# A fused attention and gated feed-forward kernel: other transfers, another order and other engines for the first four packs

## The chip, the cores and the metric

The kernel runs on one core of a Trainium2 chip. That core has a matrix engine (TensorE, PE in the profile), three engines for elementwise work (VectorE or DVE, ScalarE or ACT, GpSimd or POOL), a queue engine that only issues transfers (SyncE, SP), and 16 DMA engines. ScalarE and GpSimd can issue transfers too. Each engine takes its instructions in the order in which they stand in its program and waits at the first one whose semaphores are not there yet. The metric is the device time of one execution in microseconds; smaller is better.

## The reference, cut to what matters

The inputs are q, k and v (8 sequences, 8 heads, 576 positions, 64 values) and three weight matrices. Half of the heads see the last 32 positions, the other half every fourth of the last 128. The result of the attention is the input x of a gated feed-forward network, all in float32.

```python
def _attn_ref(q, k, v) -> np.ndarray:
    ...
    window = 32
    dilation = 4
    ...
    mask_plain = (rel >= 0) & (rel < window)
    mask_dil = (rel >= 0) & (rel < window * dilation) & (rel % dilation == 0)
    ...
    attn = np.exp(scores)
    attn = attn / (np.sum(attn, axis=-1, keepdims=True) + 1e-09)
    return np.matmul(attn, v).astype(np.float32)

def _moe_ref(x, w_gate, w_val, w_out) -> np.ndarray:
    g = x @ w_gate
    silu = g * (1.0 / (1.0 + np.exp(-g)))
    val = x @ w_val
    return (silu * val @ w_out).astype(np.float32)
```

x has 4608 tokens of 512 values; the hidden width is 1536.

## The kernel before

**Tiling.** Tokens are cut into packs of 256 tokens and 4 heads, and three chunks of 512 tokens are made in a plain way, the rest in three larger chunks that use seven products in place of eight. A pack goes through these stages: its scores (TensorE, on top of a mask that a matmul with the identity has put there), a shift by the row maximum (VectorE), the exponential (ScalarE), a transposition on TensorE and its copy out by ScalarE, the results with v (TensorE), a division by the row sum and a 32 by 32 transposition that puts them where x lies (VectorE).

**Two parts for each number.** Matmuls of the network run on a shorter format. Each factor is split: the high part is a copy into that format (ScalarE), the low part is the number less its high part (GpSimd, `x_copy_lo` at L502, `w_split_lo` at L267, and L558 for the hidden values h). A product takes three matmuls, high by high, low by high, high by low. Weights come in 24 units of 128 by 768 numbers of 8 bytes, of which five stages make two parts: E (an exponent part, ScalarE, L225), T (a shift, ScalarE at L242 or VectorE at L245), B (the bits joined, VectorE, L252 or L255), H (the high part, ScalarE, L263), L (the low part, GpSimd, L267). Step s of the plain chunks needs units 2s and 2s + 1: 12 matmuls for the gate, 12 for the value, 12 of the step before for the output.

**The first four packs.** They have functions of their own (`first_...`). Their q takes both head halves in turn over the 128 partitions; their k and v lie in places of double width that are cleared, half by half, before the rows of one half are written into them, so that one matmul serves both halves. `first_qk` issues three transfers for a pack: q over 128 partitions, and k for each half over 64. `first_v` issues two.

**What sets the order.** The loads of this stage stand in one block, and the engine that clears and the one that issues are named in the calls. The work of the first packs and of the first weight units is a list of tokens, which each engine gets in that order: a letter names the stage, a number the pack, or for W the weight stage (W0 is E, W4 is L, each on the next unit). Q is scores, S shift, X exponential, T transposition, K its copy, A results, N division, U the 32 by 32 transposition, H and L the two parts of x, Y and Z dummy matmuls. After the list the steps of the plain chunks follow; their order is laid down by the program's text and by a scheduler that reads it. At most 8 transfers of SP and ACT together are under way in this stage: each one's semaphore is that of the eighth before it, and it waits for that one to land.

Of the kernel before, what the change touches and what calls it, by code (L numbers as in the profile page):

```python
# [18 lines left out]
P = 128  # L19
# [96 lines left out]
def attention_moe(ctx, tc, qkb, vb, w, masks, ident, out):  # L116
# [3 lines left out]
    def pk(m):  # L120
        return PACKS[m]
# [143 lines left out]
    def w_split_lo(u):  # L265
        hi, lo = w_place(u)
        nc.gpsimd.tensor_tensor(out=lo, in0=wst.pop(u).bitcast(F32), in1=hi, op=ALU.subtract)  # L267
# [10 lines left out]
    def w_one(c):  # L278
        u = done[c]
        done[c] += 1  # L280
        if c == "E":
            w_exp(u)
        elif c == "T":
            w_shift(u)
        elif c == "B":
            w_bits(u)
            while ready["w"] and w_load():
                pass
        elif c == "H":
            w_split_hi(u)  # L290
        else:
            w_split_lo(u)
# [7 lines left out]
    FQ = max(2 * x.cols - FQN for x in PACKS[:4])  # L300
# [8 lines left out]
    for k, n in (("qk", FQ), ("v", 8 * FG * (D + 1))):  # L309
        early[k] = Ring(n, *range(o, o + 4 * n, n))  # L310
        o += 4 * n
# [188 lines left out]
    def x_copy_lo(m):  # L500
        h, l = x_parts(m)
        nc.gpsimd.tensor_tensor(out=l, in0=x_place(m), in1=h, op=ALU.subtract)  # L502
# [97 lines left out]
    with tc.manual_schedule(engines={et.SP, et.Pool, et.DVE, et.Activation}):  # L600
# [406 lines left out]
def layout(q, k, v, moe_w_gate, moe_w_val, moe_w_out):  # L1007
# [4 lines left out]
    for m, pk in enumerate(PACKS):  # L1012
        for (g, h), t in pk.blocks.items():
# [37 lines left out]
```

## Time and profile before

| | |
|---|---|
| median of 3 runs | 911.01 us (910.01 to 911.1) |
| the profiled execution | 910.72 us, of which the span of the program is 908.9 us |
| busy: PE, DVE, ACT, POOL | 898.4, 651.6, 375.0, 272.3 us |
| granted TensorE clock | 1.00 |
| DMA moved | 203.90 MB, 224 GB/s over the span |

The profile is of one execution, and its times are microseconds from the start of the span. Four kinds of answers are used: the busy time of each engine in stretches of the span; the timeline of one engine (start, duration, engine, line, operation, what it writes and reads, shapes, count, and in brackets how long the engine was idle before and what it waited for); the waits by engine and line; and the chain that ended last, followed back from the last instruction. `fs` is the bank of scores, `fk` and `ek` those of transposed rows, `fr` and `er` those of results, `bg`, `bv` and `bo` those of the gate, the value and the output. A DVE instruction of 0.96 us on 128 by 768 elements is one stage of a weight unit.

### The profile page before, as it was taken

The numbers are of one execution on the slowest core, as the hardware profiler recorded it, in microseconds if no ns is written. First come the engines' busy times: TensorE is split into PE (matmuls) and PEld (weight loads), VectorE is DVE, ScalarE is ACT, GpSimd is POOL, SyncE is SP. The second block draws the span as 40 slices with busy tenths as digits, with TensorE's granted clock in tenths as the row PEclk, the third lists the DMA queues.
The fourth block names the chain that finished last, engine by engine and source line by source line (L and its number), as shares of the span: only waits on it lengthen the run. The fifth ranks groups of instructions, "written<-read, shape, count | busy, mean of one in ns | idle before, by whom it ended". The sixth has DMA issues, their size and how long they took to land.

```text
span 908.9 us, 19519 instructions
## 1 busy us (share of the span) xinstructions
PE 898.4 (99%) x8082; PEld 732.1 (81%) x8082; DVE 651.6 (72%) x1014; ACT 375.0 (41%) x593; POOL 272.3 (30%) x311
## 2 busy tenths in 40 slices
PE   8899999999999999999999999999999999999998
PEld 5588888888888878888888888888888888888886
DVE  7766638788797983776689966677699746556963
ACT  6776623322333242333345543333354533334451
POOL 4766531231111122232333121232333213333310
PEclk9999999999999999999999999999999999999999
DMA  9975416776696765787777878777776776666672
GB/s 347 353 254 225 155 50 205 242 246 243 207 320 231 238 227 181 251 257 225 226 222 227 259 233 258 222 234 243 238 208 200 226 230 199 188 196 198 186 220 104
DMA packets 72553, 203.90 MB, mean 224 GB/s; under 512 B 7408, under 2 KB 21744, under 8 KB 72464
## 3 DMA queue, kind: packets, MB, share of 16 engines
q0 software_dynamic: 27520, 100.16, 36.7%
q1 hardware_dynamic: 35728, 66.32, 20.4%
q10 hardware_dynamic: 9216, 36.17, 11.7%
q8 instruction: 64, 1.05, 0.5%
q14 instruction: 25, 0.20, 0.1%
HBM read 160.15 MB, written 42.47 MB: 223 GB/s over the span
## 4 chain that ended last, share of the span: by engine, by line
PE 89%; DVE 4%; DMA 3%; issue 1%; SPq 1%; ACT 1%; POOL 1%; DVEq 0%; ACTq 0%; POOLq 0%
PE bo L853 33%; PE bv L853 12%; PE bg L853 12%; PE bo L566 9%; PE bg L517 9%; PE bv L517 9%; PE two L454 2%; PE two L414 2%; DMA pieces<-at_float32r 2%; PE two L440 1%; DMA at_int<-w 1%; DMA at_float<-vb 1%; SPq L752 0%; DVE at_float32r L744 0%; DVE at_float L730 0%
## 5 line engine op out<-in xcount | busy, mean ns | idle before, releaser
L853 PE MATMUL bo<-at_float32r 128*128 128x512 f32 x1296 | 307.5, 391 | 0.0
L853 PEld LDWEIGHTS bo<-at_float32r 128*128 128x128 f32 x1296 | 242.1, 188 | 50.9
L782 POOL DMA_DIRECT2D at_float32r<-pieces x189 | 101.6, 538 | 358.5 <-PE bo L853 223.0
L816 DVE TENSOR_TENSOR at_float<-bo,at_float 128x512 f32<-128x512 f32 (+1 forms) x169 | 113.4, 683 | 100.0 <-ACT at_float L858 59.2
L816 DVE TENSOR_TENSOR at_float32r<-at_float,at_float32r 128x512 fp32r<-128x512 f32 (+1 forms) x147 | 110.8, 778 | 31.5 <-ACT at_float32r L843 24.1
L853 PE MATMUL bg<-at_float32r 128*128 128x512 f32 x486 | 128.8, 391 | 0.0
L853 PE MATMUL bv<-at_float32r 128*128 128x512 f32 x486 | 128.8, 391 | 0.0
L566 PE MATMUL bo<-at_float32r,at_float32r 128*128 128x512 f32 x432 | 105.7, 393 | 0.8 <-POOL at_float32r L558 0.4
L558 POOL TENSOR_TENSOR at_float32r<-at_float,at_float32r 128x512 fp32r<-128x512 f32 x36 | 51.7, 1437 | 182.5 <-PE bo L566 120.6
L853 PEld LDWEIGHTS bv<-at_float32r 128*128 128x128 f32 x486 | 90.6, 188 | 19.0
L853 PEld LDWEIGHTS bg<-at_float32r 128*128 128x128 f32 x486 | 90.6, 188 | 18.7
L517 PE MATMUL bg<-at_float32r,at_float32r 128*128 128x512 f32 x420 | 102.7, 393 | 0.9 <-POOL at_float32r L267 0.5
L843 ACT CAST at_float32r<-at_float 128x512 fp32r<-128x512 f32 x126 | 75.7, 622 | 65.6 <-PE bo L853 16.2
L517 PE MATMUL bv<-at_float32r,at_float32r 128*128 128x512 f32 x420 | 102.7, 393 | 0.0
L566 PEld LDWEIGHTS bo<-at_float32r,at_float32r 128*128 128x128 f32 x432 | 80.1, 188 | 18.5 <-POOL at_float32r L558 0.8
L517 PEld LDWEIGHTS bg<-at_float32r,at_float32r 128*128 128x128 f32 x420 | 77.8, 188 | 18.3 <-DVE at_float L543 1.0
L517 PEld LDWEIGHTS bv<-at_float32r,at_float32r 128*128 128x128 f32 x420 | 77.8, 188 | 16.5
L879 ACT ACTIVATE at_float<-at_float 128x512 f32<-128x512 f32 x72 | 45.5, 632 | 93.0 <-DVE at_float L816 93.0
L858 ACT COPY at_float<-bg 128x512 f32<-128x512 f32 x63 | 37.0, 587 | 91.3 <-PE bg L853 91.1
L543 DVE SCALAR_TENSOR_TENSOR at_float<-at_float,bg 128x512 f32<-128x512 f32 x36 | 24.6, 682 | 58.8 <-ACT at_float L538 49.5
L816 POOL TENSOR_TENSOR at_float<-at_float,at_float 128x512 f32<-128x512 f32 x36 | 50.8, 1410 | 23.8 <-DVE at_float L882 20.3
L881 DVE SCALAR_TENSOR_TENSOR at_float<-at_float,at_float 128x512 f32<-128x512 f32 x72 | 49.4, 687 | 11.6 <-ACT at_float L879 11.5
(85 smaller groups left out, 882.4 us busy)
## 6 DMA issues: line engine op xcount, KB each, us to landing
at_float32r<-pieces POOLq DMA_DIRECT2D x189, 512.0 KB, 4.5
pieces<-at_float32r SPq DMA_DIRECT2D x126, 256.0 KB, 3.3
at_int<-w SPq DMA_DIRECT2D x24, 768.0 KB, 7.5
at_float<-vb ACTq DMA_DIRECT2D x31, 520.0 KB, 5.1
at_float<-qkb ACTq DMA_DIRECT2D x16, 640.0 KB, 7.0
out<-at_float SPq DMA_DIRECT2D x35, 256.0 KB, 4.2
at_float<-qkb ACTq DMA_DIRECT2D x15, 576.0 KB, 6.2
at_float<-vb SPq DMA_DIRECT2D x6, 260.0 KB, 8.2
```

The lines of the kernel that those rows point to most:

```text
L414: nc.tensor.matmul(out=two[BQ * j:BQ * j + BQ, h, a + w * g:a + w * g + w], lhsT=t[r, q:q + BQ], rhs=t[r, k:k + w], start=not masked, stop ...
L517: last["g", which] = nc.tensor.matmul(out=bank.rearrange("p (n c) -> p n c", n=2), lhsT=wcol(f, o, low), rhs=x[l][j], start=n == 0, stop=n ...
L543: last["h"] = nc.vector.scalar_tensor_tensor(out=t, in0=t, scalar=1.0, in1=bank_g[:, :CH], op0=ALU.add, op1=ALU.mult)
L558: last["l"] = nc.gpsimd.tensor_tensor(out=hl, in0=hst[i][0], in1=hst[i][1], op=ALU.subtract)
L566: nc.tensor.matmul(out=bank_o[j][:, :CH], lhsT=wcol(f, 2 * DM + P * j, low), rhs=x, start=f == 0 and low == 0 and x is hh, stop=f == NF - ...
L782: nc.gpsimd.dma_start(out=taken[asked], in_=pieces[asked % NPIECE])
L816: engine.tensor_tensor(out=out, in0=a, in1=b, op=op)
L843: nc.scalar.copy(out=o[:, 0], in_=src)
L853: nc.tensor.matmul(out=bank, lhsT=w, rhs=x, start=first and n == 0 and t in FRESH, stop=last and n == len(ops) - 1, skip_group_check=True)
L858: nc.scalar.copy(out=kept[KEPT[t]][r], in_=banks[0][r][:, :CS])
L879: nc.scalar.activation(out=f, in_=g, func=AF.Tanh, scale=0.5)
L881: nc.vector.scalar_tensor_tensor(out=f, in0=f, scalar=1.0, in1=g, op0=ALU.add, op1=ALU.mult)
```

## The change

Four things change, all in the first stage.

1. *Joined transfers.* The host lays q beside k for one half and k beside q for the other, so that one row of a half holds both, and the place is as wide as both. `first_qk` issues two transfers for a pack, of 64 partitions and 1152 or 1280 columns, in place of three. The place's columns between belong to q of both halves; the k columns of the other half are cleared as before. The same bytes are moved.
2. *Who clears and who issues.* Clears are calls of their own (`first_clear`), by VectorE and GpSimd, ahead of the transfers. The second half of q and k is issued by ScalarE (before: GpSimd for packs 0 to 2, SP for pack 3), the second half of v by GpSimd for all packs (before: SP for packs 2 and 3). ScalarE clears one half instead of four, and issues the identity that SP issued.
3. *Low parts.* Those of x for packs 2 and 3 (token D) and of the first two weight units (token V) are made by VectorE.
4. *The list of tokens* is written anew.

```diff
-    def first_qk(m, zero, engine):
-
-        t, n = early["qk"](), pk(m).cols
-        k = n - FN
-        tk = t[:, FN:FN + 2 * k].rearrange("p (h c) -> p h c", h=2)
-        nc.sync.dma_start(out=t[:, :FN], in_=qkb[m, :, :FN])
+    def first_clear(what, m, by):
+
+        k = pk(m).cols - FN
+        t = early[what](2 * (k + FN) if what == "qk" else None).rearrange("p (h c) -> p h c", h=2)
         for h in range(2):
-            clear(tk[:, h], zero[h])
-            (nc.sync, engine)[h].dma_start(out=tk[h::2, h], in_=qkb[m, D * h:D * h + D, FN:n])
-        st[m]["qk"] = t[:, :FN], tk
+            clear(t[:, h, :k] if what == "qk" else t[:, h], by[h])
+        st[m][what] = t
+
+    def first_qk(m, engine):
+
+        t, k = st[m]["qk"].rearrange("p h c -> p (h c)"), pk(m).cols - FN
+        for h in range(2):
+            engine[h].dma_start(out=t[h::2, k * h:k * h + FN + k], in_=qkb[m, D * h:D * h + D, :FN + k])
+        st[m]["qk"] = t[:, k:k + FN], st[m]["qk"]
...
-    def x_copy_lo(m):
+    def x_copy_lo(m, engine=nc.gpsimd):
         h, l = x_parts(m)
-        nc.gpsimd.tensor_tensor(out=l, in0=x_place(m), in1=h, op=ALU.subtract)
+        engine.tensor_tensor(out=l, in0=x_place(m), in1=h, op=ALU.subtract)
...
-        first_qk(0, (dve, pool), pool)
         nc.scalar.dma_start(out=consts[:, :near], in_=masks[:, :near])
-        first_qk(1, (dve, pool), pool)
-        nc.sync.dma_start(out=ident32, in_=ident)
+        for m in range(3):
+            first_clear("qk", m, (dve, pool))
+        first_qk(0, (sp, act))
+        first_qk(1, (sp, act))
         nc.scalar.activation(out=some, in_=some, func=AF.Exp)
 
         idle(WARM)
-        first_qk(2, (dve, pool), pool)
-        first_v(0, (dve, pool), pool)
-        first_qk(3, (dve, act), sp)
-        first_v(1, (dve, pool), pool)
+        first_qk(2, (sp, act))
+        nc.scalar.dma_start(out=ident32, in_=ident)
+        for m in range(2):
+            first_clear("v", m, (dve, pool))
+            first_v(m, (sp, pool))
+        first_clear("qk", 3, (dve, pool))
+        first_qk(3, (sp, act))
         w_load()
-        first_v(2, (dve, act), sp)
-        first_v(3, (act, act), sp)
+        for m in range(2, 4):
+            first_clear("v", m, ((dve, act)[m - 2], pool))
+            first_v(m, (sp, pool))
         w_load()
...
-        "L": x_copy_lo, "Y": idle, "Z": lambda n: idle(n, s_banks[0]), "W": lambda n: w_one(STAGES[n]),
+        "L": x_copy_lo, "D": lambda m: x_copy_lo(m, nc.vector), "V": lambda n: w_one(STAGES[n], nc.vector),
+        "Y": idle, "Z": lambda n: idle(n, s_banks[0]), "W": lambda n: w_one(STAGES[n]),
...
-        for what in ("Q0 S0 Q1 Y2 S1 X0 Q2 X1 T0 S2 T1 K0 K1 Q3 X2 A0 T2 K2 S3 X3 N0 A1 W0 U0 T3 K3 N1 A2 W1 U1 H0 L0 H1 L1 "
-                     "W2 Z2 A3 N2 W3 W4 U2 W0 Z3 H2 L2 N3 W1 U3 H3 L3 W2 W0 W3 W4 W0 W1 W2 W3 W4").split():
+        for what in ("Q0 S0 Q1 X0 S1 Q2 T0 K0 S2 X1 A0 T1 X2 N0 K1 T2 U0 K2 A1 H0 L0 N1 Q3 U1 S3 Z3 H1 L1 W0 X3 T3 W1 A2 K3 N2 W2 Z2 A3 "
+                     "W3 U2 W0 Z3 N3 V4 H2 W1 U3 D2 H3 W2 W0 D3 W3 V4 W0 W1 W2 W3 W4").split():
```

How this moves instructions, at the three places of which the prediction speaks.

TensorE from the third pack's scores on, before (L362 are scores, L440 transpositions, L380 results; each row's first name is the bank, `fk` or `fr` for even packs, `ek` or `er` for odd ones):

```order
L362 MATMUL fs_109<-at_2048_float_146 32x128 x16
L440 MATMUL fk<-at_128_float_59,at_512_float_216 128x128 x4
L440 MATMUL ek<-at_128_float_59,at_512_float_239 128x128 x4
L358 LDWEIGHTS at_1056_bfloat_58
L358 MATMUL fs_113<-at_1056_bfloat_58 128x512
L362 MATMUL fs_113<-at_2048_float_157 32x128 x16
L380 MATMUL fr<-at_2080_float_152,at_512_float_216 32x130 x16
L440 MATMUL fk<-at_128_float_59,at_512_float_265 128x128 x4
L380 MATMUL er<-at_2080_float_163,at_512_float_239 32x130 x16
L440 MATMUL ek<-at_128_float_59,at_512_float_313 128x128 x4
L380 MATMUL fr<-at_2080_float_170,at_512_float_265 32x130 x16
```

The same piece now (L364 scores, L442 transpositions, L382 results):

```order
L364 MATMUL fs_109<-at_2560_float_129 32x128 x16
L442 MATMUL fk<-at_128_float_59,at_512_float_212 128x128 x4
L382 MATMUL fr<-at_2080_float_149,at_512_float_212 32x130 x16
L442 MATMUL ek<-at_128_float_59,at_512_float_234 128x128 x4
L442 MATMUL fk<-at_128_float_59,at_512_float_259 128x128 x4
L382 MATMUL er<-at_2080_float_154,at_512_float_234 32x130 x16
L360 LDWEIGHTS at_1056_bfloat_58
L360 MATMUL fs_113<-at_1056_bfloat_58 128x512
L364 MATMUL fs_113<-at_2560_float_159 32x128 x16
```

Results of pack 0 stand ahead of the transposition of pack 1, and the scores of pack 3 behind the results of pack 1. Three dummy matmuls, the transposition of pack 3 and the results of pack 2 follow.

VectorE from the bits of the first weight unit on, before (L388 to L390 are the division, L487 the 32 by 32 transposition, L252 the bits of a unit, L245 and L255 shift and bits of the third):

```order
L252 SCALAR_TENSOR_TENSOR at_776_int_367<-at_1536_int_168 128x3x256
L388 TENSOR_SCALAR at_8_float_317<-fr 128x8
L389 RECIPROCAL at_8_float_317<-at_8_float_317 128x8
L390 TENSOR_TENSOR at_512_float_318<-fr,at_8_float_317 128x512
L487 STREAM_TRANSPOSE at_512_float_400<-at_512_float_318 128x2x4x2x32
L388 TENSOR_SCALAR at_8_float_346<-er 128x8
L389 RECIPROCAL at_8_float_346<-at_8_float_346 128x8
L390 TENSOR_TENSOR at_512_float_347<-er,at_8_float_346 128x512
L487 STREAM_TRANSPOSE at_512_float_413<-at_512_float_347 128x2x4x2x32
L252 SCALAR_TENSOR_TENSOR at_776_int_411<-at_1536_int_180 128x3x256
L245 TENSOR_SCALAR at_776_int_423<-at_1536_int_183 128x3x256
L255 SCALAR_TENSOR_TENSOR at_776_int_423<-at_1536_int_183,at_776_int_423 128x3x256
```

The same piece now:

```order
L252 SCALAR_TENSOR_TENSOR at_776_int_353<-at_1536_int_164 128x3x256
L489 STREAM_TRANSPOSE at_512_float_396<-at_512_float_285 128x2x4x2x32
L390 TENSOR_SCALAR at_8_float_315<-er 128x8
L391 RECIPROCAL at_8_float_315<-at_8_float_315 128x8
L392 TENSOR_TENSOR at_512_float_316<-er,at_8_float_315 128x512
L267 TENSOR_TENSOR at_1536_float32r<-at_776_int_353,at_1536_float32r 128x768
L489 STREAM_TRANSPOSE at_512_float_409<-at_512_float_316 128x2x4x2x32
L504 TENSOR_TENSOR at_2048_float32r<-at_512_float_396,at_2048_float32r 128x512
L252 SCALAR_TENSOR_TENSOR at_776_int_407<-at_1536_int_176 128x3x256
L504 TENSOR_TENSOR at_2048_float32r<-at_512_float_409,at_2048_float32r 128x512
L267 TENSOR_TENSOR at_1536_float32r<-at_776_int_407,at_1536_float32r 128x768
L245 TENSOR_SCALAR at_776_int_420<-at_1536_int_179 128x3x256
```

Four low parts (L267 and L504) stand between, the division of pack 2 has moved ahead of the first unit's bits, and, ahead of this piece, the shift of pack 3 stands behind the transposition of pack 1, where before it stood ahead of the division of pack 0.

GpSimd's low parts, before (L502 of x, L267 of weight units, L558 of h):

```order
L502 TENSOR_TENSOR at_2048_float32r<-at_512_float_369,at_2048_float32r 128x512
L267 TENSOR_TENSOR at_1536_float32r<-at_776_int_367,at_1536_float32r 128x768
L502 TENSOR_TENSOR at_2048_float32r<-at_512_float_400,at_2048_float32r 128x512
L502 TENSOR_TENSOR at_2048_float32r<-at_512_float_413,at_2048_float32r 128x512
L267 TENSOR_TENSOR at_1536_float32r<-at_776_int_411,at_1536_float32r 128x768
L267 TENSOR_TENSOR at_1536_float32r<-at_776_int_423,at_1536_float32r 128x768
L267 TENSOR_TENSOR at_1536_float32r<-at_776_int_367,at_1536_float32r 128x768
L267 TENSOR_TENSOR at_1536_float32r<-at_776_int_411,at_1536_float32r 128x768
L558 TENSOR_TENSOR at_512_float32r<-at_512_float_216,at_512_float32r 128x512
```

And now:

```order
L504 TENSOR_TENSOR at_2048_float32r<-at_512_float_337,at_2048_float32r 128x512
L267 TENSOR_TENSOR at_1536_float32r<-at_776_int_420,at_1536_float32r 128x768
L267 TENSOR_TENSOR at_1536_float32r<-at_776_int_353,at_1536_float32r 128x768
L560 TENSOR_TENSOR at_512_float32r<-at_512_float_212,at_512_float32r 128x512
L267 TENSOR_TENSOR at_1536_float32r<-at_776_int_407,at_1536_float32r 128x768
```

After pack 1 the next unit is the third, and h of the first step stands ahead of the fifth unit, where it stood behind it. From the fifth step on, all engines have the same order as before.

More of the change, by code (lines that the diff above doesn't have):

```diff
@@ L263, in w_split_hi, with w_split_lo @@
         nc.scalar.copy(out=w_place(u)[0], in_=wst[u].bitcast(F32))
-    def w_split_lo(u):
+    def w_split_lo(u, engine):
         hi, lo = w_place(u)
-        nc.gpsimd.tensor_tensor(out=lo, in0=wst.pop(u).bitcast(F32), in1=hi, op=ALU.subtract)
+        engine.tensor_tensor(out=lo, in0=wst.pop(u).bitcast(F32), in1=hi, op=ALU.subtract)
     ready = {"w": False}
@@ L276, in w_upto, with w_one @@
                 w_one(c)
-    def w_one(c):
+    def w_one(c, lows=nc.gpsimd):
         u = done[c]
@@ L291, in w_one @@
         else:
-            w_split_lo(u)
+            w_split_lo(u, lows)
     st = [{} for _ in range(NPK)]
-    FQ = max(2 * x.cols - FQN for x in PACKS[:4])
+    FQ = [2 * x.cols for x in PACKS[:4]]
     FG = NG
@@ L308, in attention_moe @@
     o = M_W + 16 * WU
-    for k, n in (("qk", FQ), ("v", 8 * FG * (D + 1))):
-        early[k] = Ring(n, *range(o, o + 4 * n, n))
-        o += 4 * n
+    for k, n in (("qk", FQ), ("v", [8 * FG * (D + 1)] * 4)):
+        early[k] = Ring(n[0], *[o + sum(n[:m]) for m in range(4)])
+        o += sum(n)
     assert o <= M_LATE
@@ L335, in clear, with first_v @@
             by.memset(x, 0.0)
-    def first_qk(m, zero, engine):
-        t, n = early["qk"](), pk(m).cols
-        k = n - FN
-        tk = t[:, FN:FN + 2 * k].rearrange("p (h c) -> p h c", h=2)
-        nc.sync.dma_start(out=t[:, :FN], in_=qkb[m, :, :FN])
-        for h in range(2):
-            clear(tk[:, h], zero[h])
-            (nc.sync, engine)[h].dma_start(out=tk[h::2, h], in_=qkb[m, D * h:D * h + D, FN:n])
-        st[m]["qk"] = t[:, :FN], tk
-    def first_v(m, zero, engine):
-        n = 4 * FG * (D + 1)
-        t = early["v"]().rearrange("p (h c) -> p h c", h=2)
-        for h in range(2):
-            clear(t[:, h], zero[h])
-            (nc.sync, engine)[h].dma_start(out=t[h::2, h], in_=vb[m, D * h:D * h + D, :n])
+    def first_clear(what, m, by):
+        k = pk(m).cols - FN
+        t = early[what](2 * (k + FN) if what == "qk" else None).rearrange("p (h c) -> p h c", h=2)
+        for h in range(2):
+            clear(t[:, h, :k] if what == "qk" else t[:, h], by[h])
+        st[m][what] = t
+    def first_qk(m, engine):
+        t, k = st[m]["qk"].rearrange("p h c -> p (h c)"), pk(m).cols - FN
+        for h in range(2):
+            engine[h].dma_start(out=t[h::2, k * h:k * h + FN + k], in_=qkb[m, D * h:D * h + D, :FN + k])
+        st[m]["qk"] = t[:, k:k + FN], st[m]["qk"]
+    def first_v(m, engine):
+        t = st[m]["v"]
+        for h in range(2):
+            engine[h].dma_start(out=t[h::2, h], in_=vb[m, D * h:D * h + D, :4 * FG * (D + 1)])
         st[m]["v"] = t.rearrange("p h (g c) -> p h g c", c=D + 1)
@@ L1016, in layout @@
             r = D * h
-            rq = slice(h, P, 2) if m < 4 else slice(r, r + D)
+            qo, ko = (pk.cols - FQN, 0) if m < 4 and h == 0 else (0, FQN)
             for j in range(NH):
-                n, i, kc = NH * pk.kind + j, NH * g + j, FQN + pk.kcol[g, j]
-                qkb[m, rq, BQ * i:BQ * i + BQ] = q[n, t].T
+                n, i, kc = NH * pk.kind + j, NH * g + j, ko + pk.kcol[g, j]
+                qkb[m, r:r + D, qo + BQ * i:qo + BQ * i + BQ] = q[n, t].T
                 qkb[m, r:r + D, kc + a:kc + BK] = k[n, kt[a:]].T
```

## The prediction

> **What bounds the kernel now.** I read the busy time by stage first, then the list of waits of TensorE (PE) after the first stage, then the chain that ended last, then the timelines of the engines in the first 42 us. Columns of the first view: stretch, its length, then busy us (and instructions) of PE, weight loads, VectorE (DVE), ScalarE (ACT), GpSimd (POOL), the granted clock, DMA share, GB/s. The last line is the only wait of PE between 41 us and 908 us.
>
> ```profile
> 0.00:41.44 41.44, 34.98 (x355) 22.38 (x355) 31.55 (x45) 27.34 (x39) 24.75 (x25) 1.00 0.97 373
> 41.44:100.00 58.56, 58.56 (x664) 47.91 (x665) 35.30 (x49) 41.97 (x59) 39.81 (x24) 1.00 0.62 217
> 100.00:200.00 100.00, 100.00 (x1099) 82.11 (x1085) 71.81 (x117) 34.20 (x53) 29.52 (x19) 1.00 0.54 182
> ...
> PE bg L517 <- DVE at_float L543: 0.4, 1, 0.4
> ```
>
> From 41.44 us on, when the gate and value matmuls of step 2 start, PE has no hole until the end but one of 0.4 us. So the end moves with the moment at which PE reaches that point, one to one, and the whole case is the first 41 us. There the chain is work on weights, not matmuls:
>
> ```profile
> 14.74 9.83 DMA at_int<-w
> ...
> 37.38 1.73 POOL at_float32r L267
> 39.11 1.25 POOL at_float32r L558
> ```
>
> The timeline shows why. GpSimd makes every low part (x at L502, weights at L267, h at L558), and from 20.22 to 32.09 it never rests; the tenfold gate group of step 1 starts 0.05 us after its second unit's end, and the first output matmuls stall twice more, on h's high part (late on ScalarE) and on h's low part, which stands behind a weight unit on GpSimd:
>
> ```profile
> 20.22 2.81 POOL L502 TENSOR_TENSOR at_float32r<-at_float,at_float32r 128x512 fp32r<-128x512 f32 x2 [11.11 <-ACT at_float32r L498]
> 22.98 1.75 POOL L267 TENSOR_TENSOR at_float32r<-at_int,at_float32r 128x768 fp32r<-128x768 f32 x1
> 24.69 3.26 POOL L502 TENSOR_TENSOR at_float32r<-at_float,at_float32r 128x512 fp32r<-128x512 f32 x2
> 27.90 4.19 POOL L267 TENSOR_TENSOR at_float32r<-at_int,at_float32r 128x768 fp32r<-128x768 f32 x2
> ...
> 32.14 2.56 PE L517 MATMUL bg<-at_float32r,at_float32r 128*128 128x512 f32 x10 [0.51 <-POOL at_float32r L267]
> 34.54 2.91 PE L517 MATMUL bv<-at_float32r,at_float32r 128*128 128x512 f32 x12
> 37.87 2.11 PE L566 MATMUL bo<-at_float32r,at_float32r 128*128 128x512 f32 x8 [0.42 <-ACT at_float32r L553]
> 40.40 1.19 PE L566 MATMUL bo<-at_float32r,at_float32r 128*128 128x512 f32 x4 [0.42 <-POOL at_float32r L558]
> ```
>
> From 32.14 PE has 34 matmuls to 41.44. At 2.73 us for 12 they need 7.7 us, so 1.6 us of the 9.3 are stalls.
>
> **The change, part by part.** Below, packs are 0 to 3, weight units u0 to u5.
>
> Transfers. Three loads of q and k per pack become two of 288 or 320 KB, none of them through GpSimd. Rows for the landing (KB each, us from issue):
>
> ```profile
> at_float<-qkb SPq DMA_DIRECT2D x4, 256.0 KB, 4.6
> at_bfloat<-masks ACTq DMA_DIRECT2D x1, 192.0 KB, 3.4
> ```
>
> The first half may be issued only after its clear, at 1.6 us (0.74 before), the other at 1.4 us. With 3.4 us as the fast and 4.6 us as the slow end, pack 0 lands between 5.0 and 6.2 us. PE is not free before 5.4 (nine dummy matmuls and a mask matmul, unchanged). I take 5.4, nearer the fast end, since both halves now run on rings that hold little else: 0.95 us ahead of the 6.35 in the next fence. Packs 1 and 2 (576 and 640 KB, 1.6 and 1.8 us at the 373 GB/s of the first stretch) come at 7.0 and some 9.2, a few tenths ahead of PE. Up to u1's load SP issues 10 transfers instead of 18, ScalarE 6 instead of 1; all six stand before ScalarE's first exponential, where it has only clears to do. Two halves of v move to GpSimd's queue and are issued by 11 us; GpSimd's first low part comes at 15.6. So the queues cost nothing on the path, and from pack 3 on landings are over 1 us ahead of use: u2, landed at 14.74 + 9.83 = 24.6 before, is wanted at 27.2 now. If that cover were gone, a late landing would count in full.
>
> The pack phase. Durations that I need, one row of each kind:
>
> ```profile
> 6.35 1.93 PE L362 MATMUL fs<-at_float 128*32 128x128 f32 x32 [0.91 <-DMA at_float<-qkb]
> 8.76 1.65 PE L362 MATMUL fs<-at_float 128*32 128x128 f32 x32
> 10.78 0.38 PE L358 MATMUL fs<-at_bfloat 128*128 128x512 bf16 x1
> 11.09 1.08 PE L362 MATMUL fs<-at_float 128*32 128x128 f32 x32
> 12.10 0.66 PE L440 MATMUL fk<-at_float,at_float 128*128 128x128 f32 x4
> 14.44 1.10 PE L380 MATMUL fr<-at_float,at_float 128*32 128x130 f32 x32
> ...
> 13.37 0.59 ACT L444 COPY at_float<-ek 128x512 f32<-128x512 f32 x1
> 13.85 0.63 ACT L436 ACTIVATE at_float<-at_float 128x512 f32<-128x512 f32 x1
> ...
> 14.70 0.69 DVE L368 TENSOR_REDUCE at_float<-fs 128x8 f32<-128x512 f32 x1 [1.04 <-PE fs L362]
> 15.43 0.69 DVE L369 TENSOR_TENSOR at_float<-fs,at_float 128x512 f32<-128x512 f32 x1
> 18.95 0.71 DVE L487 STREAM_TRANSPOSE at_float<-at_float 128x512 f32<-128x512 f32 x1
> 20.54 0.16 DVE L388 TENSOR_SCALAR at_float<-fr 128x8 f32<-128x8 f32 x1
> 20.73 0.20 DVE L389 RECIPROCAL at_float<-at_float 128x8 f32<-128x8 f32 x1
> 20.97 0.69 DVE L390 TENSOR_TENSOR at_float<-fr,at_float 128x512 f32<-128x512 f32 x1
> 21.70 1.13 DVE L487 STREAM_TRANSPOSE at_float<-at_float 128x512 f32<-128x512 f32 x1
> ```
>
> I walk the new order with them: a hand-off between engines takes 0.05 us, and an instruction that waits for nothing starts 0.08 us before the one ahead of it ends, as the starts show. Scores 0: 5.4 to 7.4. Scores 1 (mask matmul, then 1.65): 9.4. Scores 2 (1.39 with its mask): 10.7. Turn 0: 11.3, its copy: 11.9, results 0: 13.1. Turn 1: 13.6, copy 14.2, results 1: 15.4. Norm 1 on VectorE (1.12): 16.6, turn of y 1: 17.6 (between 0.71 and 1.13: GpSimd is on pack 0's low part). Only now comes shift 3 (1.4): 19.0, though its scores are done at 16.9; before, it stood ahead of norm 0. Exponential 3: 19.6, turn 3: 20.4, and results 2, which PE holds behind turn 3: 21.3. Norm 2, which waits for them, began at 20.54 before and begins at 21.4 now. So the early start is spent, and 0.8 us more, before the weights are reached.
>
> The weights. VectorE now has norm 2, u0's bits, y 2, norm 3, low u0, y 3, low x2, u1's bits, low x3, low u1, u2's shift and bits, in that order and with hardly a gap:
>
> ```profile
> 19.66 0.96 DVE L252 SCALAR_TENSOR_TENSOR at_int<-at_int 128x768 int32<-128x768 int32 x1
> 24.79 2.02 DVE L252 SCALAR_TENSOR_TENSOR at_int<-at_int 128x768 int32<-128x768 int32 x1
> 26.72 0.94 DVE L245 TENSOR_SCALAR at_int<-at_int 128x768 int32<-128x768 int32 x1
> ...
> L816 DVE TENSOR_TENSOR at_float32r<-at_float,at_float32r 128x512 fp32r<-128x512 f32 (+1 forms) x147 | 110.8, 778 | 31.5 <-ACT at_float32r L843 24.1
> ...
> 21.90 0.92 ACT L225 ACTIVATE at_int<-at_int 128x768 f32<-128x768 f32 x1 [0.41 <-DMA at_int<-w]
> 28.80 0.83 ACT L263 CAST at_float32r<-at_int 128x768 fp32r<-128x768 f32 x1 [0.31 <-DVE at_int L255]
> 29.53 0.59 ACT L538 ACTIVATE at_float<-bg 128x512 f32<-128x512 f32 x1
> ```
>
> A low part on VectorE has no row at this place. For 768 elements the bounds are 0.96 (same shape, two operands in SBUF, GpSimd idle) and 2.02 (GpSimd at work, as for u1 here); I take 0.96, because GpSimd has nothing to do between pack 1's low part (done at 19.7) and u2's. For 512 elements: 0.64 (0.96 scaled) to 0.78 (the group at L816), taken as 0.69. That adds 2 x 0.96 + 2 x 0.69 = 3.3 us to VectorE and takes 6.8 us from GpSimd; what VectorE gets back, since u1's bits and two turns of y no longer meet GpSimd, is 1.06 + 2 x 0.42 = 1.9 us. From 21.3: norm 2 to 22.5, the rest 9.4 (their sum less the overlaps, with 0.2 of waiting for u1's high part), so u2's bits end at 31.9; before, its high part started right behind them at 28.80. ScalarE now has tanh 0 (0.59), u3's shift and u4's exponent part (0.9 each) ahead of u2's high part, which so ends at 33.1 and not at 32.7; low u2 on GpSimd (1.75 and a hand-off): 34.9, where it was 32.09.
>
> From there PE runs through. h's low part now stands ahead of u4's, h's high part ahead of u4's, so both stalls are gone: 34.9 + 7.8 = 42.75 against 41.44. The same walk over the old order gives 41.5, so it can be trusted to some tenths. Lost 2.8 at u2, regained 1.6 of stalls: **+1.3 us**. Engine orders after the first stage are the same, so nothing follows. On the profiled execution's own 910.72 us (a span of 908.9 and 1.8 around it) that is 912.0; the median of the three runs shown, 911.01, lies 0.3 higher, so I predict **912.3**.
>
> **Rivals.** *A, slower beyond doubt: pack 0's joined transfers land at the slow end.* Place: PE's first score matmul. For: their issue waits for a clear, and the slow end is the median of the old loads of that size. Against: those stood behind others on one ring, the new ones stand first. At 6.2 us instead of 5.4 everything slides by 0.8 to 0.9, since nothing later on the walk has slack up to u2: 42.75 + 0.9, so 913.2. It decides from a landing of 5.9 us on. *B, faster: VectorE is not the bound, the landing of u1 is.* u1 came at 21.9; a microsecond less is 20.9. If shift 3 does not hold results 2 back and VectorE is free for it, 20.9 + exponent 0.92 + shift 0.9 + bits 0.96 + high 0.83 + low 0.96 + u2's shift and bits 1.9 + high 0.83 + low 1.75 is 30.3 with hand-offs; PE would reach step 2 at 38.1, 3.3 us early: 907.7. It decides if norm 2 begins by 18. Against it: the order stands in each engine's program, and PE cannot pass turn 3. *C, no change:* pack 2 lands by 8 us and the first two score groups run at the pace of the third; the walk then gives 42.0 and 911.6. *D, PE slows in the hole.* Between scores 3 (16.8) and turn 3 (19.7) PE now has 0.7 us of dummies and 2.2 us of nothing. The same mask matmul took 0.63 us at 4.81 and 0.38 at 10.78, though the granted clock reads 1.00:
>
> ```profile
> 4.81 0.63 PE L358 MATMUL fs<-at_bfloat 128*128 128x512 bf16 x1
> ```
>
> So PE has a slow pace, and turn 3 and results 2 at that pace (times 0.63/0.38) would cost 0.4 + 0.7 more: 913.4. [...]
>
> **How the numbers follow.** Forecast 912.3, chance 0.45, own range 911.3 to 913.2; A 0.20, D 0.08, C 0.15, B 0.12. Leaving out B and the outer edge of A and D gives the range 909.6 to 914.2. A measurement here tells 0.2%, 1.8 us, from no change. Faster by that (under 909.2): B, 0.12. Slower (over 912.8): 0.10 of the forecast's 0.45 and most of A and D, 0.32 in all. The rest, 0.56, is within it.
>
> **What would show it.** Score matmuls start at 5.4 (A: 6.2); results 2 of PE end at 21.3, about 1.4 us later than before; VectorE has no idle time from there to 32; u2's low part on GpSimd ends near 35; output matmuls of step 0 run without a stall; step 2 starts at 42.75 and PE keeps its one hole of 0.4 us. I am wrong if VectorE waits for the landing of u1, or if PE shows new holes after 43 us.

## The result: 5 us slower, and the profile after

The changed kernel takes 916.18 us (median of 6 runs, 915.89 to 917.43), the kernel before beside it 911.06 (910.01 to 912.66): ratio 1.0056, 95% interval 1.0046 to 1.0066. A second comparison on another chip gave 1.0064 (1.0051 to 1.0077). The forecast was 912.3, the range ended at 914.2. The profiled execution took 916.11 us, its span is 914.3.

PE's timeline up to step 2 (L364 scores of packs 0 to 2, L442 a turn, which is a transposition, L382 results, L528 gate and value of step 0, L519 of step 1 and later, L416 scores of a later pack, L568 the output):

```profile
6.50 1.08 PE L364 MATMUL fs<-at_float 128*32 128x128 f32 x32 [1.06 <-DMA at_float<-qkb]
...
7.97 1.08 PE L364 MATMUL fs<-at_float 128*32 128x128 f32 x32
...
9.66 1.08 PE L364 MATMUL fs<-at_float 128*32 128x128 f32 x32 [0.18 <-issue]
11.49 0.63 PE L442 MATMUL fk<-at_float,at_float 128*128 128x128 f32 x4 [0.75 <-DMA at_float<-ident]
...
20.42 0.66 PE L442 MATMUL ek<-at_float,at_float 128*128 128x128 f32 x4 [1.87 <-ACT at_float L438]
21.00 1.09 PE L382 MATMUL fr<-at_float,at_float 128*32 128x130 f32 x32
...
31.37 1.07 PE L528 MATMUL bv<-at_float32r,at_float32r 128*128 128x512 f32 x4
34.52 0.73 PE L519 MATMUL bg<-at_float32r,at_float32r 128*128 128x512 f32 x2 [2.08 <-ACT at_float32r L263]
35.18 0.32 PE L416 MATMUL two<-at_float 64*32 64x64 f32 x10
36.34 4.15 PE L519 MATMUL bg<-at_float32r,at_float32r 128*128 128x512 f32 x10 [0.84 <-POOL at_float32r L267]
40.33 2.90 PE L519 MATMUL bv<-at_float32r,at_float32r 128*128 128x512 f32 x12
43.07 2.88 PE L568 MATMUL bo<-at_float32r,at_float32r 128*128 128x512 f32 x12
45.79 0.39 PE L519 MATMUL bg<-at_float32r,at_float32r 128*128 128x512 f32 x1
```

Step 2 starts at 45.79 us; it was 41.44 before, and 42.75 in the prediction. Both stalls at the output matmuls are gone, as predicted: the rows at 40.33 and 43.07 follow without a hole. But the ten gate matmuls at 36.34 take 4.15 us, and the same ten took 2.56 before. The busy time by stretches (columns as before: PE, weight loads, VectorE, ScalarE, GpSimd, then the granted clock, DMA share, GB/s) says why:

```profile
30.05:33.46 3.41, 2.10 (x8) 1.43 (x8) 3.11 (x4) 2.95 (x5) 0.00 (x0) 1.00 1.02 416
33.46:36.88 3.42, 1.52 (x14) 0.94 (x15) 3.42 (x5) 3.42 (x6) 2.34 (x2) 1.00 0.84 284
36.88:40.29 3.41, 3.41 (x9) 2.65 (x8) 2.65 (x2) 1.88 (x3) 3.41 (x2) 0.50 0.91 359
40.29:43.70 3.41, 3.41 (x16) 2.80 (x15) 1.12 (x2) 3.07 (x5) 3.41 (x3) 1.00 0.89 347
```

For 3.41 us PE was granted half its clock, right behind a stretch of 3.42 us in which it was busy for 1.52.

VectorE's timeline (L371 the second half of a shift, L390 the begin of a division, L489 the 32 by 32 transposition, L267 a weight's low part, L245 and L255 shift and bits of u2) and, behind the dots, GpSimd's:

```profile
19.00 0.69 DVE L371 TENSOR_TENSOR at_float<-fs,at_float 128x512 f32<-128x512 f32 x1
22.16 0.17 DVE L390 TENSOR_SCALAR at_float<-fr 128x8 f32<-128x8 f32 x1 [2.48 <-PE fr L382]
...
24.07 1.10 DVE L489 STREAM_TRANSPOSE at_float<-at_float 128x512 f32<-128x512 f32 x1
...
26.95 1.08 DVE L489 STREAM_TRANSPOSE at_float<-at_float 128x512 f32<-128x512 f32 x1
...
30.32 0.96 DVE L267 TENSOR_TENSOR at_float32r<-at_int,at_float32r 128x768 fp32r<-128x768 f32 x1 [0.30 <-ACT at_float32r L263]
31.19 0.95 DVE L245 TENSOR_SCALAR at_int<-at_int 128x768 int32<-128x768 int32 x1
32.17 0.96 DVE L255 SCALAR_TENSOR_TENSOR at_int<-at_int,at_int 128x768 int32<-128x768 int32 x1
...
34.54 4.17 POOL L267 TENSOR_TENSOR at_float32r<-at_int,at_float32r 128x768 fp32r<-128x768 f32 x2 [14.15 <-ACT at_float32r L263]
```

VectorE stands idle for 2.48 us ahead of norm 2 and then works up to u2's bits with no pause over 0.30 us. GpSimd, which does u2's low part (the first of the two at 34.54), has been idle for 14.15 us by then.

The 5.4 us between the two spans (914.3 and 908.9) are 4.35 at the start of step 2 and 1.0 later. Behind step 2 the engines' orders are the same and PE waits nowhere. From there to PE's last matmul it is 864.22 us, 863.80 before, and 863.03 to 864.41 over all fourteen profiled executions of this study; these 0.4 us lie within that scatter. From PE's last matmul to the end of the span it is 4.32 us, 3.70 before. These 0.6 us are no scatter: a second profile of the change has 4.32 again, the two runs below with other low parts in the kernel before have 3.69, the joined transfers alone 3.87 and the low parts alone 4.13. They come with the change, at the very end of the program, and their cause is open.

In one thing the two profiles differ by chance. The scores of packs 0 and 1 take 1.08 us each here, 1.93 and 1.65 before. In the trace the first record of a granted clock stands at 6.16 us here and at 9.98 before; ahead of its first record a view prints 1.00 for want of any. The change is not what makes the difference: the run with five dummy matmuls has the changed kernel's own first stage (its edit comes later in PE's order), and there the scores of pack 0 take 1.93 us:

```profile
6.46 1.93 PE L364 MATMUL fs<-at_float 128*32 128x128 f32 x32 [1.01 <-DMA at_float<-qkb]
```

There norm 2 starts at 23.00 instead of 22.16.

### The profile page after: what moved, and what is told of

Same layout as the page of the kernel before. It is cut to its first block, busy times and chain, and to the rows that moved or that the text cites. A ratio compares the mean times of both kernels' runs of the same rounds, so it can differ in the third digit from the quotient of the medians.

```text
span 914.3 us, 19506 instructions
## 1 busy us (share of the span) xinstructions
PE 899.7 (98%) x8083; PEld 732.9 (80%) x8083; DVE 652.5 (71%) x1018; ACT 372.0 (41%) x590; POOL 267.5 (29%) x309
## 4 chain that ended last, share of the span: by engine, by line
PE 96%; DMA 1%; ACT 1%; DVE 1%; issue 0%; POOL 0%; DVEq 0%; ACTq 0%; POOLq 0%
PE bo L861 32%; PE bv L861 12%; PE bg L861 12%; PE bo L568 11%; PE bg L519 11%; PE bv L519 11%; PE two L456 3%; PE two L416 2%; PE two L442 2%; DMA at_float<-ident 1%; DVE at_float L489 0%; ACT at_int L225 0%; PE fr L382 0%; POOL at_float32r L267 0%; ACT at_float32r L263 0%
## 5 line engine op out<-in xcount | busy, mean ns | idle before, releaser
L519 PE MATMUL bg<-at_float32r,at_float32r 128*128 128x512 f32 x420 | 104.4, 398 | 2.9 <-ACT at_float32r L263 2.1
L568 PE MATMUL bo<-at_float32r,at_float32r 128*128 128x512 f32 x432 | 105.5, 393 | 0.0
L519 PE MATMUL bv<-at_float32r,at_float32r 128*128 128x512 f32 x420 | 102.9, 394 | 0.0
L519 PEld LDWEIGHTS bg<-at_float32r,at_float32r 128*128 128x128 f32 x420 | 78.9, 190 | 20.4 <-ACT at_float32r L263 2.5
L568 PEld LDWEIGHTS bo<-at_float32r,at_float32r 128*128 128x128 f32 x432 | 80.3, 188 | 17.1
L519 PEld LDWEIGHTS bv<-at_float32r,at_float32r 128*128 128x128 f32 x420 | 78.0, 188 | 16.7
```

The source lines that it names most:

```text
L519: last["g", which] = nc.tensor.matmul(out=bank.rearrange("p (n c) -> p n c", n=2), lhsT=wcol(f, o, low), rhs=x[l][j], start=n == 0, stop=n ...
L568: nc.tensor.matmul(out=bank_o[j][:, :CH], lhsT=wcol(f, 2 * DM + P * j, low), rhs=x, start=f == 0 and low == 0 and x is hh, stop=f == NF - ...
```

## The experiments

Two theories stood against each other. **Theory**: low parts on VectorE stand ahead of u2's bits there, VectorE is the bound, and the hole in which PE waits for it halves PE's clock. **Rival**: transfers that land later (pack 3's at 14.8 us, the identity's at 11.36) are the loss. Each run's ratio is to the kernel before on the same chip, whose median was 910.1 to 910.4 us. The mean clock of an execution is the granted clock averaged over its span.

**Joined transfers alone.** The changed kernel with the list of tokens of the kernel before.

```diff
-        for what in ("Q0 S0 Q1 X0 S1 Q2 T0 K0 S2 X1 A0 T1 ...
+        for what in ("Q0 S0 Q1 Y2 S1 X0 Q2 X1 T0 S2 T1 K0 K1 Q3 ...
```

> The joined transfers alone: transfers of the changed kernel, with the order of work of the kernel before and every low part on GpSimd. Theory (the loss is VectorE's added low parts plus a halved TensorE clock behind the gate group of step 0): the first two score groups run at the fast pace, but pack 3 lands at 14.8 us instead of 13.4, VectorE takes its shift ahead of norm 0, and everything behind slides by 1.2 us: u2's low part ends at 33.4 (32.1 before), step 2 starts at 42.8, clock 1.00 throughout, 912.2 us. Rival (late landings, the identity's above all, are the loss): most of the 5.1 us is here, 914 to 916 us.

912.66 us, ratio 1.0027 (1.0014 to 1.0039). In the profiled execution (912.28) pack 3's shift starts at 15.84 instead of 14.70, and step 2 at 42.50, 1.06 us late; the clock is 1.00. Its rows for VectorE and PE:

```profile
15.84 0.69 DVE L370 TENSOR_REDUCE at_float<-fs 128x8 f32<-128x512 f32 x1 [2.19 <-PE fs L364]
...
42.50 0.85 PE L519 MATMUL bg<-at_float32r,at_float32r 128*128 128x512 f32 x3
```

The theory's number holds in that execution, but not its first step: the scores of packs 0 and 1 took 1.94 and 1.69 us there, close to the 1.93 and 1.65 of before. The other five went up to 915.02, with mean clocks of 0.996 to 0.998, and the median lies 2.2 us over that of before where 1.2 was expected. So the transfers cost something by themselves, short of the rival's 914 to 916.

**Low parts alone.** The kernel before with the four low parts on VectorE, at their places.

```diff
-  ... W2 Z2 A3 N2 W3 W4 U2 W0 Z3 H2 L2 N3 W1 U3 H3 L3 W2 W0 W3 W4 W0 ...
+  ... W2 Z2 A3 N2 W3 V4 U2 W0 Z3 H2 D2 N3 W1 U3 H3 D3 W2 W0 W3 V4 W0 ...
```

> The low parts alone: the kernel before with the four low parts (x of packs 2 and 3, weight units 0 and 1) on VectorE, at the places where they stood; transfers and the other order as before. Theory: VectorE gets 3.3 us more in front of u2's bits, u2's low part ends at 36.4 instead of 32.1, both stalls at the output matmuls go, step 2 starts at 44.3: 913.9 us, and 915.5 if the TensorE clock halves in the longer hole as well. Rival (late landings are the loss): u2's low part at 32 to 33, 911 us.

916.10 us, ratio 1.0062 (1.0047 to 1.0077): as much as the whole change loses, with none of the new transfers or the new order. (The losses of the parts do not add up to that of the change.) Step 2 starts at 47.41, 44.3 expected at full clock. The clock is halved for four stretches running, the first of which stands here (busy time by stretches):

```profile
25.51:28.92 3.41, 1.54 (x7) 0.72 (x6) 2.69 (x4) 1.43 (x2) 0.00 (x0) 1.00 1.01 412
28.92:32.34 3.42, 2.33 (x6) 1.85 (x7) 2.49 (x4) 1.88 (x3) 0.00 (x0) 0.50 1.03 418
```

u2's low part (the first of the two in this row of GpSimd's timeline) ends at 36.85:

```profile
35.10 4.16 POOL L267 TENSOR_TENSOR at_float32r<-at_int,at_float32r 128x768 fp32r<-128x768 f32 x2 [11.65 <-ACT at_float32r L263]
```

**The changed kernel with its low parts back on GpSimd.**

```diff
-  ... W0 Z3 N3 V4 H2 W1 U3 D2 H3 W2 W0 D3 W3 V4 W0 W1 W2 W3 W4
+  ... W0 Z3 N3 W4 H2 W1 U3 L2 H3 W2 W0 L3 W3 W4 W0 W1 W2 W3 W4
```

> The changed kernel with its transfers and its order, but the four low parts back on GpSimd. Theory: GpSimd fills its idle 20.4 to 34.5 us, u2's bits end at 30.7, its low part at 33.9 instead of 36.3, the hole of TensorE is shorter and the clock stays at 1.00, step 2 starts at 41.9 instead of 45.8: 911.4 us. Rival (late landings): within 0.5 us of the changed kernel, 916.

912.05 us, ratio 1.0022 (1.0013 to 1.0032). Against 1.0056 and 1.0064 the low parts on VectorE cost 3.1 to 3.8 us; transfers and order together 2.0 and not the 0.4 expected. The rival is out as the main cause: with landings as late (the identity's at 12.05 us) most of the loss is gone. The profiled execution, one of the slower ones with 913.39, missed its marks: u2's bits end at 32.77, not 30.7, and step 2 starts at 44.55, not 41.9. PE's clock halved in the pack phase there, behind a stretch with 1.32 us of work, and norm 2 began only at 24.04 (busy time by stretches, and PE's timeline):

```profile
10.84:14.25 3.41, 1.32 (x31) 1.11 (x32) 1.38 (x2) 1.34 (x3) 0.00 (x0) 1.00 1.03 416
14.25:17.67 3.42, 3.42 (x40) 2.64 (x36) 1.77 (x4) 1.57 (x4) 0.00 (x0) 0.50 1.02 417
```

```profile
36.14 2.56 PE L519 MATMUL bg<-at_float32r,at_float32r 128*128 128x512 f32 x10 [0.50 <-POOL at_float32r L267]
...
44.55 3.01 PE L519 MATMUL bg<-at_float32r,at_float32r 128*128 128x512 f32 x12 [0.37 <-DVE at_float L545]
```

What the low parts add to VectorE's chain can be read all the same. From the start of norm 2 to the end of u2's bits it takes 8.7 us here, 11.0 in the change, 8.2 before and 12.5 in the low parts alone.

**Five dummy matmuls in the hole.**

```diff
             gv_first()
+            with behind("q"):
+                idle(5, bank_o[0])
```

> The changed kernel with five dummy matmuls of 512 columns on TensorE between the gate and value group of step 0 and the gate group of step 1, where it waits from 32.44 to 34.52 us (five take 1.95 us). Theory (the low clock follows from the hole): the granted clock stays at 1.00, ten matmuls of step 1's gate take 2.6 us instead of 4.2, step 2 starts at 44.2: 914.5 us. Rival (those ten are slow for another reason, operands or memory shared with VectorE and GpSimd): 4.2 us still, 916.2 us.

914.61 us, ratio 1.0042 (1.0025 to 1.0059): the number fits, but its profile does not. A dummy takes 0.22 us behind another and not 0.39 (the five took 1.25 us in a row), so the five filled 1.1 us of the hole, and the clock halved all the same (busy time by stretches; the dummies write a bank that the output matmuls write over later):

```profile
33.95:37.36 3.41, 1.58 (x16) 0.60 (x14) 3.41 (x6) 3.41 (x5) 1.94 (x2) 1.00 0.76 254
37.36:40.77 3.41, 3.41 (x9) 2.63 (x10) 3.04 (x2) 1.91 (x4) 3.41 (x2) 0.50 0.86 306
```

**Twelve of them.** The same edit with `idle(12, ...)`.

> The changed kernel with twelve dummy matmuls in the hole of TensorE instead of five: at 0.22 us each they cover 32.4 to 35.2 us, so that no window of 3.4 us (the length of each stretch at half clock) is less than half busy. Theory (a window less than half busy halves the clock for the next): clock 1.00 throughout after 10 us, step 2 starts 1.6 us earlier than in the changed kernel, 914.5 us. Rival (ten matmuls slow for another reason): the clock still reads 0.50 in them, 916 us.

In the profiled execution the theory holds: the stretch at the hole is busy for 2.56 of 3.41 us, the clock reads 1.00 in it and in the next, the ten matmuls take 2.57 us, and step 2 starts at 44.38 instead of 45.79. The stretch, and the row of PE's timeline:

```profile
33.30:36.71 3.41, 2.56 (x12) 1.25 (x11) 3.41 (x5) 3.41 (x5) 1.99 (x2) 1.00 0.82 265
```

```profile
36.53 2.57 PE L519 MATMUL bg<-at_float32r,at_float32r 128*128 128x512 f32 x10 [0.85 <-POOL at_float32r L267]
```

That execution took 914.61 us. The other three took 915.48 to 915.90 with mean clocks of 0.997 and 0.998, and the ratio is 1.0060 (1.0044 to 1.0075), no better than the change. So the hole at 32.4 us seems not to be the only place; the last run below takes this up.

**Results 2 ahead of turn 3.**

```diff
-  ... Q3 U1 S3 Z3 H1 L1 W0 X3 T3 W1 A2 K3 N2 ...
+  ... Q3 U1 S3 Z3 A2 H1 L1 W0 X3 N2 T3 W1 K3 ...
```

> The changed kernel with the results of pack 2 ahead of the turn of pack 3 on TensorE, and norm 2 ahead of it on VectorE (five names of the list moved). Theory (VectorE is the bound and loses 2.48 us waiting for results 2 at 19.69 to 22.16 us): norm 2 starts near 20, u2's bits end at 31.4 instead of 33.1, step 2 starts at 44.0 with the halved clock and at 42.4 without: 914.3 or 912.7 us. Rival (late landings of the weights hold the chain): u2's bits move by less than 0.5 us, 916 us.

914.33 us, ratio 1.0046 (1.0032 to 1.0059), as the theory has it with the halved clock. Norm 2 starts at 20.13 instead of 22.16, step 2 at 43.85, and the ten matmuls still take 4.14 us (timelines of VectorE and PE):

```profile
20.13 0.17 DVE L390 TENSOR_SCALAR at_float<-fr 128x8 f32<-128x8 f32 x1 [0.47 <-PE fr L382]
...
34.42 4.14 PE L519 MATMUL bg<-at_float32r,at_float32r 128*128 128x512 f32 x10 [1.10 <-POOL at_float32r L267]
```

**Other low parts, in another place.** The kernel before with the low parts of u1 and u2 on VectorE, behind u2's bits; and the same with h's low part ahead of u4's on GpSimd (the second piece of the diff, in that run alone).

```diff
-  ... H3 L3 W2 W0 W3 W4 W0 W1 W2 W3 W4
+  ... H3 L3 W2 W0 W3 W0 W1 W2 V4 W3 V4
...
-        w_upto(L=W + 3, H=W + 4 - (s == 0))
+        w_upto(L=W + 3 - (s == 1), H=W + 4 - (s == 0))
+        with behind(*["l"] * (s == 1)):
+            w_upto(L=W + 3)
```

> The kernel before with the low parts of weight units 1 and 2 (not 0 and 1, and none of x) on VectorE, and both behind u2's bits there, where VectorE is idle from 28.76 to 30.16 us. Theory (a low part on VectorE costs only where it stands ahead of u2's bits): u2's low part ends at 30.8 instead of 32.1, step 2 starts at 40.7 instead of 41.4: 0.7 us faster than before, ratio 0.9992. Rival (low parts on VectorE cost by themselves, wherever they stand): 0.5 us or more slower than before.

> As the run before it in this list, and on GpSimd the low part of h of step 0 ahead of the low part of weight unit 4, as in the changed kernel. Theory: the second stall at the output matmuls goes as well, step 2 starts at 40.0: 1.4 us faster than before, ratio 0.9985. Rival (that stall is not the end of the chain): as the run before it.

909.20 us, ratio 0.9988 (0.9980 to 0.9997), and 908.57 us, ratio 0.9983 (0.9974 to 0.9992): a little faster than both kernels. The instruction itself takes as long as ahead of the bits, 0.97 us a piece below against 0.95 and 0.96. What differs is where it stands, and also that two low parts moved here and four there. Rows of the second one, for VectorE (both low parts in the row at 28.56) and PE:

```profile
27.57 1.07 DVE L255 SCALAR_TENSOR_TENSOR at_int<-at_int,at_int 128x768 int32<-128x768 int32 x1
28.56 1.94 DVE L267 TENSOR_TENSOR at_float32r<-at_int,at_float32r 128x768 fp32r<-128x768 f32 x2
...
31.15 3.02 PE L517 MATMUL bg<-at_float32r,at_float32r 128*128 128x512 f32 x12 [0.86 <-DVE at_float L543]
34.01 2.88 PE L517 MATMUL bv<-at_float32r,at_float32r 128*128 128x512 f32 x12
36.93 3.01 PE L566 MATMUL bo<-at_float32r,at_float32r 128*128 128x512 f32 x12
39.78 2.43 PE L517 MATMUL bg<-at_float32r,at_float32r 128*128 128x512 f32 x10
```

u2's low part is ready before PE asks for it, all twelve gate matmuls run together, and step 2 starts at 39.78 (expected 40.0).

**The identity issued early.** On SP behind pack 0's half.

```diff
+        nc.sync.dma_start(out=ident32, in_=ident)
         first_qk(1, (sp, act))
...
-        nc.scalar.dma_start(out=ident32, in_=ident)
```

> The changed kernel with the identity's transfer issued on SP right behind pack 0's half, instead of on ScalarE behind pack 2's. Theory (turn 0 waits for it): it lands by 9 us instead of 11.36, turn 0 starts right behind scores 2 at 10.8 instead of 11.49, results 2 end 0.5 to 0.7 us earlier, u2's low part ends at 35.8 instead of 36.3; ratio to before 1.0050 where the changed kernel has 1.0056. Rival (the wait is taken up by a later one, u0's landing at 18.13): results 2 and the time do not move.

A miss: 916.92 us, ratio 1.0073 (1.0056 to 1.0089). Turn 0 no longer waits for the identity, but pack 1's half, now behind it on SP, lands at 9.36 us instead of 7.83, PE waits for that (PE's timeline):

```profile
9.49 1.93 PE L364 MATMUL fs<-at_float 128*32 128x128 f32 x32 [1.82 <-DMA at_float<-qkb]
```

and in the stretch around it PE is busy for 1.40 of 3.42 us; in the next, from 8.99 to 12.40 us, the granted clock reads 0.50 (busy time by stretches):

```profile
5.57:8.99 3.42, 1.40 (x33) 0.94 (x33) 2.83 (x4) 1.20 (x2) 2.90 (x5) 1.00 1.02 378
```

So whether turn 0's wait can be had back for nothing is left open.

**The change with its low parts elsewhere.** Its transfers and order, results 2 ahead of turn 3, low parts and h as in the fastest run above.

```diff
-  ... S3 Z3 H1 L1 W0 X3 T3 W1 A2 K3 N2 ... N3 V4 H2 W1 U3 D2 H3 W2 W0 D3 W3 V4 W0 W1 W2 W3 W4
+  ... S3 Z3 A2 H1 L1 W0 X3 N2 T3 W1 K3 ... N3 W4 H2 W1 U3 L2 H3 W2 W0 L3 W3 W0 W1 W2 V4 W3 V4
```

> The changed kernel's joined transfers and its order, with results 2 ahead of turn 3, the low parts of x and u0 on GpSimd, those of u1 and u2 on VectorE behind u2's bits, and h's low part ahead of u4's. Theory (the place of the low parts and the wait for results 2 are the whole loss; transfers and order do no harm): u2's low part ends near 30.7, step 2 starts near 40.1, ratio 0.9984, as good as the same low parts in the kernel before (0.9983). Rival (the joined transfers cost 1 us by themselves, by their spread of landings): ratio 0.9995 or more.

909.35 us, ratio 0.9992 (0.9983 to 1.0002); step 2 starts at 40.18, as expected. Against the change, 0.64 to 0.72% of the time, some 6 us, hang on which low parts VectorE and GpSimd make and when, and on one place in PE's order. Against the same low parts in the kernel before, the new transfers and order still lose 0.8 us; the theory's number (0.9984) and the rival's (0.9995) both lie within the interval, and this last difference is not settled.

**No holes.** The change as it is, and the change with dummy matmuls wherever PE waits up to step 1 (28 more, not the 31 that the expectation says).

```diff
-    WARM = 9
+    WARM = 11
...
-  ... Q2 T0 K0 S2 ... U1 S3 Z3 H1 ...
+  ... Q2 Y3 T0 Y3 K0 S2 ... U1 S3 Z9 Z2 H1 ...
...
+            with behind("q"):
+                idle(12, bank_o[0])
```

> The changed kernel as it is, as the measure for the run beside it on the same chip: 5.1 us over before, ratio 1.0056, mean clock 0.998 or less in every execution. If its ratio is under 1.004, the comparisons with the first measurement above have to be read anew.

> The changed kernel with 31 more dummy matmuls on TensorE, put where it waits up to step 1: two before the first scores, three each ahead of and behind turn 0, eleven instead of three behind scores 3, twelve behind the gate and value group of step 0. Theory (a window of 3.4 us less than half busy halves the clock of the next, and the grid of windows lies differently in each execution): no window is less than half busy wherever the grid lies, so the clock reads 0.999 or 1.000 in nearly every execution, the ten matmuls of step 1 take 2.6 us in all of them, and the time is 1.6 us under that of the changed kernel (ratio 1.0038). Rival (the low clock does not come from holes, or the dummies delay as much as they save): clock 0.998 or less again, ratio 1.005 or more.

The change: 916.37 us, mean clocks 0.993 to 0.998. Without holes: 914.02 us, ratio 1.0040 (1.0026 to 1.0054), mean clocks 0.999 and 1.000 in all five executions. So PE's clock is worth about 2.35 us of the loss, net of what the dummies themselves delay; the fastest of the five of the change (915.00) and the slowest of the five without holes (915.13) just overlap. In this execution of the change there were two such places, the earlier one in the hole at turn 3 (busy time by stretches):

```profile
18.13:21.55 3.42, 1.55 (x19) 0.87 (x21) 1.73 (x3) 2.93 (x5) 1.29 (x2) 1.00 1.03 414
21.55:24.96 3.41, 3.41 (x54) 2.08 (x50) 1.97 (x5) 0.40 (x2) 0.00 (x0) 0.50 1.01 410
...
31.79:35.20 3.41, 1.46 (x7) 0.85 (x5) 3.38 (x5) 2.95 (x6) 0.00 (x0) 1.00 0.76 271
35.20:38.61 3.41, 3.07 (x16) 1.89 (x17) 3.41 (x5) 3.41 (x6) 3.27 (x2) 0.50 0.72 267
```

and without holes, in PE's timeline, the ten matmuls take 2.60 us. That profile is of the slowest of the five; its ten matmuls start later than in the change (38.02, there 36.34 and 37.14), and its step 2 starts at 45.90, where the two profiles of the change have 45.79 and 47.24. So what the dummies win shows in the times more than in this profile:

```profile
33.94 2.76 PE L599 MATMUL bo<-at_float 128*128 128x512 bf16 x12
...
38.02 2.60 PE L519 MATMUL bg<-at_float32r,at_float32r 128*128 128x512 f32 x10 [0.84 <-POOL at_float32r L267]
```

## Why the prediction was wrong

The direction and the chain were right: u2's chain over VectorE got longer, the stalls at the output went, PE waits nowhere behind step 2. Three terms of the sum were wrong, and a fourth was put at nothing.

1. **"From there PE runs through"**, and 34.9 + 7.8. This step failed. The 7.8 us are right at full pace: from the ten matmuls to step 2 it took 7.85 us with twelve dummies (36.53 to 44.38). But the prediction took full pace for granted, right behind a hole of 2.08 and one of 0.84 us, and the ten matmuls took 4.15 instead of 2.56: 1.6 us. Rival D had a slow pace behind a hole, but put it at turn 3 alone, with a chance of 0.08. There the hole was 1.87 us long in this execution and turn 3 took 0.66 us, its full pace; the two holes here left 1.52 us of work in a stretch of 3.42 us, and in the next the clock read 0.50. In a second profile of the change it read 0.50 behind the hole at turn 3 too.
2. **"Turn 0: 11.3" (its end).** It ended at 12.12, since the identity landed at 11.36. The front part told that the identity moved from SP to ScalarE, where it stands behind four other transfers; the part on the queues counted the transfers and never asked when the identity comes, because turn 0 had not waited for it before. Results 2 end at 22.10 instead of 21.3: 0.8 us. That a remedy costs elsewhere is what the early identity showed.
3. **"The rest 9.4", with 0.71 us for each transposition of y 2 and y 3.** They took 1.10 and 1.08 with GpSimd idle from 20.39 to 34.54. The 1.1 us of the rows before were put down to GpSimd; they come with packs 2 and 3 in both profiles (1.13 and 1.11 us before), and that of y 1 took 0.71 in the change (from 17.67 us on) though GpSimd was at work for part of it (until 17.94) (that the pattern of packs 2 and 3 is the cause is argued, not shown). That is 0.8 us, of which some was won back, since u2's bits ended 1.2 late in all (33.13 for 31.9) and its low part 1.4 late (36.29 for 34.9).
4. **"So nothing follows."** At the end of the program 0.6 us follow, in both profiles of the change, for a reason that is open.

Then 1.4 and 1.6 make up the 3.0 us between 42.75 and 45.79, 0.6 stand at the end, and 0.4 are scatter.

What held: low parts on VectorE take 0.95 and 0.68 us (0.96 and 0.69 taken), and both stalls went. The first half of the walk came out at scores 2 (10.74, predicted 10.7), but by luck. Pack 0 started at 6.50 and not at 5.4, at the slow end, as rival A had it; yet scores 0 and 1 ran at 1.08 us instead of 1.93 and 1.65, in an execution whose first record of the clock stands at 6.16 us and not at 9.98. In the execution shown above in which the scores of pack 0 took 1.93, A's loss came: scores 2 ended at 11.95, and norm 2 started 0.84 us later than in the first profile of the change. So the walk took its pace for the first scores from one execution of before. The same holds for D's reading of the mask matmul at 4.81, slow "though the granted clock reads 1.00": the first record of the clock stands at 9.98 us there.

B fell with the order, as argued: norm 2 began at 22.16 and not by 18. Of C's two conditions the pace of the first scores was met, by the same luck, and the landing of pack 2 (9.57, not 8) was not. The sign of the low parts could have been read in the trace of before: from 14.70 us on VectorE had next to no idle time ahead of u2's bits, and 1.4 us behind them (28.76 to 30.16), so a low part ahead of them should lose and one behind them need not. The run with two low parts behind them bears this out.

## What to carry to other kernels

Before work moves to an engine that has time on average, find the instruction on it that the end of the chain waits for, and put the work behind that instruction, not ahead; four low parts ahead of it cost 5.6 us by themselves (clock included), two others behind it gained 1.1. Price a new wait of TensorE twice: as the hole itself, and as the half pace that can follow it. Here that followed where PE was busy for 0.39 to 0.46 of a stretch of 3.41 us, and lasted one such stretch in the change and four (13.65 us) in the low parts alone. And follow every transfer that is issued from another queue or in another place to its first reader, also the one that had slack. Before two single profiles are compared, look where the first record of the clock stands in each (6.16 and 9.98 us here).

## What the runs showed of the chip

In the trace of the change the granted clock is on record as 1.00 from 6.16 to 36.88 us (30.72 us, nine times 3.41), as 0.50 to 40.29 us (3.41 us) and as 1.00 up to 914.10 us. In the other profiles that are cut into such stretches, 0.50 begins at 21.55 and 35.20 us (the second profile of the change), at 28.92 (low parts alone), 14.25 (low parts back on GpSimd), 37.36 (five dummy matmuls) and 8.99 us (the identity early). In the stretch ahead of each of these seven, PE was busy for 1.32 to 1.58 us, which is 0.39 to 0.46 of it. Cut in the same way from the first record of the clock on, the profiles of the change and of the kernel before have 23 more stretches at full clock that begin before 48 us; PE was busy for 0.52 or more of each (the least 1.79 of 3.41 us, from 9.57 us on in the change), and in the next the clock read 1.00. It read 0.50 for up to four stretches running: in the low parts alone from 28.92 to 42.58 us, with PE busy for 0.62 to 0.82 in the first three. That the busy share of a stretch decides is the author's reading. It fits the hole with five dummy matmuls (0.46, and 0.50 granted behind it) and with twelve (0.75, and 1.00 behind it); none of these stretches was busy for 0.47 to 0.51, and what would follow such a one is not shown.
